# Attention output computed with channels on partitions and turned into a mirrored token order, and a Fourier mix that reads each frequency row twice

## The chip, the cores and the metric

The kernel runs on one core of a Trainium2 chip. The metric is device time in microseconds of one execution; below, a "profile" is one execution recorded by the hardware profiler, with the start, length and releaser of every instruction. The engines are TensorE (PE; its weight loads are recorded apart, as PEld), VectorE (DVE), ScalarE (ACT), GpSimd (POOL) and SyncE (SP), which here only issues transfers. Each engine executes its own list of instructions in the order in which it stands in the program.

## What is computed

A gated linear attention over 4 batches, 8 heads, 768 tokens and 48 channels a head, followed by one FNet block on the 4 x 768 x 384 result, all in float32:

```python
f = 1.0 / (1.0 + np.exp(-f_logit))
for t in range(S):
    state = f[:, :, t, :, None] * state + np.einsum('bhd,bhe->bhde', k[:, :, t], v[:, :, t])
    y[:, :, t] = np.einsum('bhd,bhde->bhe', q[:, :, t], state)
x = y.transpose(0, 2, 1, 3).reshape(B, S, H * D)
mixed = np.real(np.fft.fft(np.fft.fft(x, axis=1), axis=2))
u = x + mixed
un = (u - mean(u)) / np.sqrt(var(u) + 1e-06)          # over the last axis
out = u + np.maximum(un @ w_ch1, 0.0) @ w_ch2         # 384 -> 1536 -> 384
```

The weights arrive as float64 and are rounded to float32 on the chip.

## The kernel before

**Units.** `attention(u, x_all)` handles two heads of one batch; there are 16 units, four for each batch. Tokens lie along the row and channels on the partitions: head 0 on partitions 0 to 47, head 1 on 64 to 111, with zeros between (so 112 rows, `R`). A unit is a generator cut by `yield` into seven pieces: (0) the gates, a chain through DVE, ACT and POOL that ends in `wq`, `wk` and the scaled Q and K; (1) `sa`, (2) `sb`, (3) `sc`, (4) `sd`: score products of blocks of growing size on TensorE, with `double` on DVE in between, which folds the decay into Q and K; POOL and ACT copy the scores into `AT`; (5) `st` and `ds`: K's chunks are transposed (L262), copied to `kT` (L265, L266), multiplied with v (L269), and a chain of five DVE operations carries the state from chunk to chunk (L272, L274), on 96 columns of which each head uses its own 48; (6) `y`: for each of six chunks of 128 tokens, scores by v (L282) and Q by state (L286) give 128 tokens x 48 channels for each head; one ACT copy (L288) brings them to `x`, where tokens lie on partitions. After that the next transfer into this unit's `qkf` buffer is issued.

**FNet.** `fnet(b, x)` handles a batch in 18 pieces. Piece 1 forms `eo`, the sums (DVE, L300) and differences (POOL, L301) of tokens s and s + 384, and folds the channels around the middle into `xf` (L304 to L306). Pieces 2 to 4 compute `z`, channel terms by frequencies 0 to 384, in three groups of 128 rows (L321, L324); ACT copies each to `zz` (L326) and DVE makes `zr`, the same columns reversed and with a sign (L328), since frequency 768 - m is the mirror of m. Pieces 5 and 6 compute `mix`, six chunks of 128 tokens by 384 channels, from `zz` for the first three and from `zr` for the last three (L337); for each chunk DVE adds it to `x` and takes the statistics of the layer norm (L339 to L342), and after every three chunks ACT computes `rstd`. Then, in two halves of three chunks: `un` (DVE), its transposes `pt` (TensorE), the copy `unT` (ACT), twelve groups `up` with ReLU (L364, L367), three groups `po` (L375), the sum (L377), and a store on SP's queue (L378).

**Order.** The loop at the end runs in ticks. A unit starts every third tick and one piece of each running unit is written per tick; then two pieces of the work `behind`: first the 24 conversions of the weights, later `fnet` of a batch whose units are all done. The framework then orders each engine's instructions by its own estimate of when they can run, so that the list is near the written order, but not the same. Rotating buffers are the rest of the coupling: two PSUM tiles for the scores (`sc`), one for `y`, two for `fnet` (`f`), three `qkf` buffers.

## Time and profile before

| what | us |
|---|---|
| median of 3 runs | 943.72 |
| lowest, highest run | 943.67, 949.11 |
| span of the profiled execution, first to last instruction | 932.4 |
| TensorE busy, 9848 instructions | 741.6 (80%) |
| VectorE busy | 396.8 (43%) |
| GpSimd busy | 233.1 (25%) |
| ScalarE busy | 203.5 (22%) |

For the profiled execution only the span is given and no time of its own; the median is 11.3 us longer than it. "Busy" adds up the recorded lengths of an engine's instructions. In rows of groups, `out<-in` names the tiles, `128*64` for a matmul the rows and columns of the stationary operand, `128x193` the moving one, and `xN` how many instructions. What stands in brackets is how long the engine sat idle before, and who ended it. In a table by stage the first pair of numbers is the stretch, then its length, then the busy time (and number of instructions) of each engine; behind them stand the granted clock of TensorE, as a share of full speed, the transfers' share and GB/s.

### The profile page before, as it was taken

The numbers are of one execution on the slowest core, as the hardware profiler recorded it, in microseconds if no ns is written. First come the engines' busy times: TensorE is split into PE (matmuls) and PEld (weight loads), VectorE is DVE, ScalarE is ACT, GpSimd is POOL, SyncE is SP. The second block draws the span as 40 slices with busy tenths as digits, with TensorE's granted clock in tenths as the row PEclk, the third lists the DMA queues.
The fourth block names the chain that finished last, engine by engine and source line by source line (L and its number), as shares of the span: only waits on it lengthen the run. The fifth ranks groups of instructions, "written<-read, shape, count | busy, mean of one in ns | idle before, by whom it ended". The sixth has DMA issues, their size and how long they took to land.

```text
span 932.4 us, 21578 instructions
## 1 busy us (share of the span) xinstructions
PE 741.6 (80%) x9848; PEld 517.6 (56%) x9848; DVE 396.8 (43%) x739; ACT 203.5 (22%) x365; POOL 233.1 (25%) x246
## 2 busy tenths in 40 slices
PE   0352514447989989978999899869899999699998
PEld 0342403346765665666656656667656656555554
DVE  5977778676671131258721411465710211340000
ACT  2412121231242131213221311213320110112020
POOL 4556485554420020025210100144110000100000
PEclk9999999999979989968989889859899999799999
DMA  9224242402200200311201102022000000000000
GB/s 175 108 69 120 69 103 74 98 2 53 53 2 1 68 11 1 69 43 21 52 1 39 40 1 55 24 53 40 3 1 9 18 1 18 9 1 1 25 1 25
DMA packets 12075, 36.31 MB, mean 39 GB/s; under 512 B 1745, under 2 KB 5073, under 8 KB 10321
## 3 DMA queue, kind: packets, MB, share of 16 engines
q1 hardware_dynamic: 11984, 34.94, 15.5%
q8 instruction: 77, 1.26, 0.6%
q14 instruction: 14, 0.11, 0.0%
HBM read 30.22 MB, written 4.72 MB: 37 GB/s over the span
## 4 chain that ended last, share of the span: by engine, by line
PE 63%; DVE 5%; ACT 4%; POOL 4%; issue 3%; POOLq 0%
PE up L364 21%; PE po L375 17%; PE y L282 5%; PE mix L337 4%; PE z L321 4%; PE y L286 2%; PE sb L187 2%; PE ds L269 2%; DVE qkf L207 1%; POOL gk L170 1%; POOL wk L176 1%; PE sa L187 1%; PE z L324 1%; PE st L262 1%; POOL eo L301 1%
## 5 line engine op out<-in xcount | busy, mean ns | idle before, releaser
L364 PE MATMUL up<-unT,w 128*128 128x384 f32 x576 | 197.8, 503 | 1.3 <-ACT unT L358 1.1
L375 PE MATMUL po<-w,h 128*128 128x384 f32 x576 | 192.1, 494 | 0.0
L364 PEld LDWEIGHTS up<-unT,w 128*128 128x128 f32 x576 | 111.2, 196 | 77.1 <-issue 6.1
L375 PEld LDWEIGHTS po<-w,h 128*128 128x128 f32 x576 | 110.5, 193 | 76.8 <-issue 3.2
L377 DVE TENSOR_TENSOR x<-po,x 128x384 f32<-128x384 f32 x24 | 13.3, 556 | 224.8 <-PE po L375 224.8
L207 DVE TENSOR_TENSOR qkf<-qkf,tl 112x384 f32<-112x384 f32 x64 | 52.3, 817 | 121.6 <-PE sb L187 95.0
L230 POOL COPY at<-ad 32x384 f32<-32x384 f32 x64 | 56.5, 883 | 164.7 <-DVE ad L192 162.7
L367 ACT ACTIVATE h<-up 128x384 f32<-128x384 f32 x96 | 47.2, 492 | 166.8 <-PE up L364 166.8
L282 PE MATMUL y<-v,at 128*128 128x48 f32 x384 | 76.0, 338 | 3.4 <-issue 3.4
L170 POOL TENSOR_TENSOR gk<-qkf 112x768 f32<-112x768 f32 x16 | 29.5, 1846 | 194.4 <-DVE qkf L160 162.3
L282 PEld LDWEIGHTS y<-v,at 128*128 128x128 f32 x384 | 66.2, 248 | 8.4 <-issue 3.7
L187 PE MATMUL sb<-qkf 48*32 48x32 f32 x3072 | 37.7, 221 | 22.5 <-DVE qkf L208 21.1
L286 PE MATMUL y<-stt,qkf 48*128 48x48 f32 x320 | 41.2, 341 | 14.9 <-DVE stt L272 9.5
L252 PE MATMUL sd<-qkf 48*64 48x64 f32 x384 | 19.1, 262 | 42.7 <-DVE qkf L208 42.7
L187 PEld LDWEIGHTS sb<-qkf 48*32 48x32 f32 x3072 | 32.7, 122 | 34.0 <-DVE qkf L208 25.9
L208 DVE TENSOR_TENSOR qkf<-qkf,tl 112x384 f32<-112x384 f32 x64 | 46.3, 724 | 0.0
L120 POOL TENSOR_TENSOR tailf<-tailf,pow 128x384 f32<-128x384 f32 x24 | 35.5, 1481 | 42.3 <-DVE pow L118 34.8
L321 PE MATMUL z<-tab,xf 128*128 128x193 f32 (+1 forms) x192 | 37.9, 372 | 8.9 <-POOL xf L306 8.9
L252 PEld LDWEIGHTS sd<-qkf 48*64 48x64 f32 x384 | 16.7, 172 | 48.3 <-issue 48.3
L286 PEld LDWEIGHTS y<-stt,qkf 48*128 48x128 f32 x320 | 30.2, 231 | 23.7 <-DVE stt L272 10.0
L176 POOL TENSOR_TENSOR wk<-wk,qkf 112x768 f32<-112x768 f32 x16 | 30.4, 1900 | 36.8 <-ACT wk L172 36.7
L288 ACT COPY x<-y 128x576 f32<-128x576 f32 x16 | 10.2, 639 | 134.3 <-PE y L286 134.3
(76 smaller groups left out, 889.4 us busy)
## 6 DMA issues: line engine op xcount, KB each, us to landing
qkf<-in_qkf_dram SPq DMA_DIRECT2D x32, 432.0 KB, 6.7
raw<-in_w_ch_dram SPq DMA_DIRECT2D x24, 384.0 KB, 3.3
v<-in_v_dram SPq DMA_DIRECT2D x16, 288.0 KB, 3.2
out_dram<-x SPq DMA_DIRECT2D x24, 192.0 KB, 1.9
tab<-in_seq_tab_dram SPq DMA_DIRECT2D x1, 1158.0 KB, 15.6
cd<-in_dim_tab_dram SPq DMA_DIRECT2D x1, 576.0 KB, 15.7
masks<-in_sel_dram SPq DMA_DIRECT2D x1, 64.0 KB, 5.8
ident<-in_ident_dram SPq DMA_DIRECT2D x1, 64.0 KB, 5.8
```

The costliest lines, as they stand in the source:

```text
L170: nc.gpsimd.tensor_tensor(blocks(gk), blocks(g), at(g, LEAF - 1), ALU.subtract)
L176: nc.gpsimd.tensor_tensor(wk, wk, K, ALU.mult)
L187: nc.tensor.matmul(ps[32 * s:32 * s + 32, r, off + 32 * c:off + 32 * c + 32], lhsT=kk[ROWS[r], o:o + 32], rhs=qq[ROWS[r], o:o + 32], start ...
L207: nc.vector.tensor_tensor(qv[:, :, 1], qv[:, :, 1], wide(tv[:, :, 0:1]), ALU.mult)
L208: nc.vector.tensor_tensor(kv[:, :, 0], kv[:, :, 0], wide(tv[:, :, 1:2]), ALU.mult)
L230: nc.gpsimd.tensor_copy(AT[rows, :, :, 32 * s:32 * s + 32], AD[rows])
L282: nc.tensor.matmul(o, lhsT=AT[:, r, c], rhs=vt[:, c, r * D:(r + 1) * D], start=True, stop=(c == 0))
L286: nc.tensor.matmul(o, lhsT=Q[ROWS[r], c * C:(c + 1) * C], rhs=st[ROWS[r], c - 1, r * D:(r + 1) * D], start=False, stop=True)
L321: nc.tensor.matmul(o, lhsT=xf[:, i, j, ch], rhs=tab[:, j, cs, cols], start=(j == 0), stop=(j == 2))
L364: nc.tensor.matmul(pp[:, :3 * 128], lhsT=w1[:, kt, m * 128:(m + 1) * 128], rhs=unT[:, kt], start=(kt == 0), stop=(kt == 2))
L367: nc.scalar.activation(h, pp[:, :3 * 128], AF.Relu)
L375: nc.tensor.matmul(po[:, :DM], lhsT=h1[m][:, i * 128:(i + 1) * 128], rhs=w2[:, m], start=(m == 0), stop=(m == NF - 1))
```

## The change

1. *States.* `ds` and `st` hold only each head's own 48 columns: two matmuls of 64 and 48 weight columns for each chunk (`FILL`), and DVE operations of 48 columns for 96. The transposes are laid at steps of 128 columns, so that one ACT copy replaces two.
2. *Output.* `y` is computed with channels on the partitions and tokens along the row: v is now the stationary operand and `AT` the moving one (128 columns), then the state is stationary and Q moves. Head 0 goes to partitions 0 to 63, head 1 to 64 to 111. Two ACT copies bring it to `yT`, the second with the tokens 385 to 767 reversed. A new piece transposes six chunks (`yt`, in the score buffers) and ACT copies them to `x`. So in `x` chunk c + 3 holds, in row p, the mirror image of the token in chunk c; the slot that would be token 768 holds token 384. A unit has eight pieces.
3. *Fourier stages.* The folded channels are two tiles, `xc` (cosines) and `xs` (sines); even and odd frequencies stand side by side, so that a matmul streams 386 columns and not 193. POOL makes a copy of one chunk of sums, in which one element is the difference. `zr` and its DVE operations go. One frequency row in the middle is a group of its own (`mid`, one weight column). Each of three `mix` groups is used twice: as it is for chunk c, and with its columns read backwards (385 columns, column 0 again at the end) for chunk c + 3. The statistics of all chunks follow behind the three groups. `fnet` has 20 pieces.
4. *Store.* The chunks 0 to 2 are stored by SP as before; the mirrored chunks 3 to 5 by an indirect transfer of POOL with a table of row numbers, `place`, that two iotas write at the start.

```diff
-        for c in range(NCH - 1):
-            nc.tensor.matmul(ps[:R, 0, c * 2 * D:(c + 1) * 2 * D], lhsT=kT[:, c], rhs=vt[:, c],
-                             start=True, stop=True)
+            for r in range(2):
+                nc.tensor.matmul(ds[FILL[r], c], lhsT=kT[:, c, FILL[r]], rhs=vt[:, c, r * D:(r + 1) * D],
+                                 start=True, stop=True)
...
         for c in range(NCH):
             for r in range(2):
-                o = y[:, r, c * D:(c + 1) * D]
-                nc.tensor.matmul(o, lhsT=AT[:, r, c], rhs=vt[:, c, r * D:(r + 1) * D],
-                                 start=True, stop=(c == 0))
...
+                nc.tensor.matmul(y[FILL[r], c * C:(c + 1) * C],
+                                 lhsT=vt[:, c, r * D:r * D + (64 if r == 0 else D)], rhs=AT[:, r, c],
+                                 start=(c % 4 == 0), stop=(c == 0), skip_group_check=True)
+        for c in range(1, NCH):
+            for r in range(2):
+                nc.tensor.matmul(y[ROWS[r], c * C:(c + 1) * C], lhsT=st[ROWS[r], c - 1],
+                                 rhs=Q[ROWS[r], c * C:(c + 1) * C], start=False, stop=True,
+                                 skip_group_check=True)
+
+        yT = p2.tile([128, S], F32, tag="yT", name=f"yT{u}")[:R]
+        nc.scalar.copy(yT[:, :HS + 1], y[:R, :HS + 1])
+        nc.scalar.copy(yT[:, HS + 1:], y[:R, S - 1:HS:-1])
+        yield
+
+        ps = ps_a.tile([128, 2, 512], F32, tag="sc", name=f"yt{u}").rearrange("p a b -> p (a b)")
+        for c in range(NCH):
+            nc.tensor.transpose(ps[:, c * 128:c * 128 + R], yT[:, c * C:(c + 1) * C], ident[:R, :R])
+        nc.scalar.copy(
+            x_all[:, :, hp * 2 * D:(hp + 1) * 2 * D].rearrange("t c (r e) -> t c r e", r=2),
+            ps[:, :NCH * 128].rearrange("t (c r k) -> t c r k", r=2, k=64)[:, :, :, :D])
...
+    def store(b, c, rows):
+        if c < 3:
+            nc.sync.dma_start(out=out[b, c * C:(c + 1) * C], in_=rows)
+        else:
+            nc.gpsimd.indirect_dma_start(
+                out=out.rearrange("b s d -> (b s) d"),
+                out_offset=bass.IndirectOffsetOnAxis(ap=place[:, b, c - 3:c - 2], axis=0),
+                in_=rows, in_offset=None)
...
+        nc.gpsimd.tensor_tensor(o, x[:, 0:3], x[:, 3:6], ALU.subtract)
+        nc.gpsimd.tensor_copy(e[:, 3], e[:, 0])
+        nc.gpsimd.tensor_copy(e[0:1, 3], o[0:1, 0])
+        nc.vector.tensor_tensor(xs[:, :, 1:HD], o[:, :, 1:HD], o[:, :, DM - 1:HD:-1], ALU.subtract)
+        nc.vector.tensor_tensor(xc[:, :, 1:HD], e[:, :, 1:HD], e[:, :, DM - 1:HD:-1], ALU.add)
+        nc.gpsimd.tensor_copy(xc[:, :, 0:HD + 1:HD], e[:, :, 0:HD + 1:HD])
...
+            parts = []
+            if T < 2:
+                ch = slice(128 * T, 128 * T + 128)
+                parts += [(z[:, :2 * NQ], xc[:, j, ch], tab[:, j, 0]) for j in (1, 2)]
+                parts += [(z[:, EV], xc[:, 0, ch], tab[:, 0, 0, EV]), (z[:, OD], xc[:, 3, ch], tab[:, 0, 0, OD])]
+            if T == 1:
+                parts += [(z[64:128, :2 * NQ], xs[:, j, 0:64], tab[:, j, 1]) for j in range(3)]
+            if T == 2:
+                parts += [(z[:, :2 * NQ], xs[:, j, 64:192], tab[:, j, 1]) for j in range(3)]
...
-            nc.vector.tensor_scalar(zr[:, T], zz[:, T, S // 2:0:-1], sgn[:, T:T + 1], None, ALU.mult)
...
+        mid = mixed(f"mid{b}", slice(HS, HS + 1), DM)
+        row = p1.tile([128, DM], F32, tag="row", name=f"row{b}")
+        nc.vector.tensor_tensor(row[0:1], mid[0:1, :DM], x[0:1, 3], ALU.add)
+        for c in range(3):
+            mix = mixed(f"mix{b}_{c}", slice(c * 128, (c + 1) * 128), DM + 1)
+            nc.vector.tensor_tensor(x[:, c], mix[:, :DM], x[:, c], ALU.add)
+            nc.vector.tensor_tensor(x[:, c + 3], mix[:, DM:0:-1], x[:, c + 3], ALU.add)
+            if c == 0:
+                nc.vector.tensor_copy(x[0:1, 3], row[0:1])
+            yield
```

Where instructions stand changes in three places. In the names the number behind the letters is the unit (`sd11`) or the batch and group (`po1_5`, `z2_0`).

TensorE before, from the last `po` instruction of batch 1 to the first rows of the products that follow:

```order
L375 MATMUL po1_5_5099<-w2_89,h1_1_1_11_4990 128x384
L252 MATMUL sd11_5114<-qkf2_82 64x64 x12
L187 MATMUL sa12_5132<-wq12_5071,wk12_5072 32x32 x48
L187 MATMUL sa12_5132<-qkf0_80 32x32 x48
L262 MATMUL st11_5234<-ident_93,qkf2_82 128x112 x5
L282 MATMUL y11_5364<-v11_4079,at1_84 128x48 x4
L269 MATMUL ds11_5243<-v11_4079,kT11_5240 112x96 x5
L187 MATMUL sb12_5255<-qkf0_80 32x32 x48
L286 MATMUL y11_5364<-stt11_5249,qkf2_82 128x48 x2
```

Then follow the rest of y11 and sb12, sc12, sd12, sa13 and z2_0. TensorE after, from the last rows of y11, whose first rows now stand right behind the last `po1_5`:

```order
L300 MATMUL y11_5474<-qkf2_82,stt11_5329 48x128 x10
L245 MATMUL sc12_5500<-qkf0_80 32x32 x24
L311 MATMUL yt11_5548<-ident_94,yT11_5497 128x112 x6
L258 MATMUL sd12_5560<-qkf0_80 64x64 x12
L193 MATMUL sa13_5578<-wq13_5535,wk13_5536 32x32 x48
L193 MATMUL sa13_5578<-qkf1_81 32x32 x48
L275 MATMUL st12_5680<-ident_94,qkf0_80 128x112 x5
L361 MATMUL z2_0_5823<-tab_91,xc_87 128x386 x2
```

sd11, sa12, st11, ds11 and sb12 no longer stand between the batches, but between `up` and `po` of batch 1: st11 and ds11 behind po1_3.

POOL before, around the difference `eo` of batch 1:

```order
L211 TENSOR_TENSOR tl9_3770<-tl9_3770 112x6
L301 TENSOR_TENSOR eo1_3873<-x1_1663 128x1152
L230 COPY at0_83<-ad0_85 32x12x32 x4
L306 COPY xf_87<-eo1_3873 128x3x2 x2
L170 TENSOR_TENSOR gk10_4118<-qkf1_81 112x768
```

POOL after:

```order
L217 TENSOR_TENSOR tl9_3860<-tl9_3860 112x6
L236 COPY at0_83<-ad0_85 32x12x32 x4
L323 DMA out_0_dram<-x0_126,place_96 3072x384 x2
L337 TENSOR_TENSOR eo1_4097<-x1_1699 128x1152
L338 COPY eo1_4097<-eo1_4097 128x384
L339 COPY eo1_4097<-eo1_4097 1x384
L342 COPY xc_87<-eo1_4097 128x4x2
L176 TENSOR_TENSOR gk10_4175<-qkf1_81 112x768
```

The copies to `at0` moved ahead of the difference, two indirect stores stand between, and two copies follow it.

DVE before, in batch 3, from the third `mix` group on:

```order
L339 TENSOR_TENSOR x3_5007<-mix3_2_6904,x3_5007 128x384
L341 BN_STATS bs3_2_6909<-x3_5007 128x6
L342 BN_AGGR mv3_6886<-bs3_2_6909 128x2
L354 TENSOR_SCALAR un3_0_6941<-x3_5007,mv3_6886,rstd3_6887 128x384
L339 TENSOR_TENSOR x3_5007<-mix3_3_6914,x3_5007 128x384
L354 TENSOR_SCALAR un3_1_6948<-x3_5007,mv3_6886,rstd3_6887 128x384
```

DVE after, from the last `mix` group on:

```order
L384 TENSOR_TENSOR x3_4994<-mix3_2_7036,x3_4994 128x384
L390 BN_STATS bs3_2_7048<-x3_4994 128x6
L390 BN_STATS bs3_3_7053<-x3_4994 128x6
L391 BN_AGGR mv3_7015<-bs3_2_7048 128x2
L390 BN_STATS bs3_4_7056<-x3_4994 128x6
L391 BN_AGGR mv3_7015<-bs3_3_7053 128x2
L390 BN_STATS bs3_5_7059<-x3_4994 128x6
L391 BN_AGGR mv3_7015<-bs3_4_7056 128x2
L403 TENSOR_SCALAR un3_0_7065<-x3_4994,mv3_7015,rstd3_7016 128x384
```

Before, the first `un` stood ahead of the last three groups of `mix`; now it stands behind the last group and four statistics.

More of the change, by code (lines that the diff above doesn't have):

```diff
@@ L41 @@
     NQ = S // 4 + 1
+    HS = S // 2
     HD = DM // 2
@@ L276, in attention @@
         yield
[L278 removed]
+        y = ps_y.tile([128, 2, 512], F32, tag="y", name=f"y{u}").rearrange("p a b -> p (a b)")
         for c in range(NCH):
             for r in range(2):
[L281 to L287 removed]
@@ L332, in fnet, with mixed @@
         rstd = p2.tile([128, NCH], F32, tag="rstd", name=f"rstd{b}")
-        for c in range(NCH):
-            mix = ps_f.tile([128, 512], F32, tag="f", name=f"mix{b}_{c}")
-            src = zz if c < 3 else zr
-            for T in range(3):
-                nc.tensor.matmul(mix[:, :DM], lhsT=src[:, T, (c % 3) * 128:(c % 3 + 1) * 128], rhs=cd[:, T],
-                                 start=(T == 0), stop=(T == 2))
-            nc.vector.tensor_tensor(x[:, c], mix[:, :DM], x[:, c], ALU.add)
+        def mixed(name, rows, n):
+            mix = ps_f.tile([128, 512], F32, tag="f", name=name)
+            for T in range(3):
+                nc.tensor.matmul(mix[:rows.stop - rows.start, :n], lhsT=zz[:, T, rows], rhs=cd[:, T, :n],
+                                 start=(T == 0), stop=(T == 2))
+            return mix
+        mid = mixed(f"mid{b}", slice(HS, HS + 1), DM)
[8 more added lines that the diff above has]
+            yield
+        for c in range(NCH):
             bs = p3.tile([128, 6], F32, tag="bs", name=f"bs{b}_{c}")
@@ L377, in fnet @@
                 nc.vector.tensor_tensor(x[:, c], po[:, :DM], x[:, c], ALU.add)
-                nc.sync.dma_start(out=out[b, c * C:(c + 1) * C], in_=x[:, c])
+                store(b, c, x[:, c])
                 yield
-    left, xs, active, behind = [HP] * B, {}, [], [weights()]
+    left, xs_of, active, behind = [HP] * B, {}, [], [weights()]
     u = tick = 0
@@ L396 @@
                 if not left[b]:
-                    behind.append(fnet(b, xs.pop(b)))
+                    behind.append(fnet(b, xs_of.pop(b)))
         for _ in range(BESIDE):
```

80 lines of the change are left out of this document (33 added, 47 removed).

## The prediction

> **What bounds the kernel now.** I read the page's first line, then a table of busy time by stage. TensorE (PE, its weight loads PEld beside it) is the engine that carries the second half, so I cut the span where its work changes kind: up to the first Fourier matmul `z` of batch 0; then for each batch from `z` to the first `up`; from `up` to the last `po`; and the gap from there to the next batch's `z`.
>
> ```profile
> span 932.4 us, 21578 instructions
> core 0: us, PE busy (x) PEld busy (x) DVE busy (x) ACT busy (x) POOL busy (x), PEclk, DMA share, GB/s
> 0.00:227.20 227.20, 87.59 (x2709) 77.73 (x2709) 169.46 (x309) 55.22 (x88) 128.41 (x123) 1.00 0.36 89
> 227.20:273.98 46.78, 44.32 (x658) 34.38 (x658) 31.21 (x62) 16.70 (x30) 13.24 (x14) 0.87 0.13 27
> 273.98:395.90 121.92, 119.35 (x1075) 75.12 (x1075) 26.51 (x52) 25.29 (x46) 13.60 (x21) 0.95 0.12 29
> 395.90:427.18 31.28, 21.46 (x732) 19.67 (x731) 21.08 (x33) 5.57 (x10) 14.08 (x13) 0.62 0.21 47
> 427.18:470.86 43.68, 40.62 (x658) 30.54 (x658) 30.29 (x60) 16.65 (x30) 12.84 (x14) 0.91 0.14 29
> 470.86:593.80 122.94, 119.95 (x1076) 75.79 (x1076) 26.51 (x52) 25.32 (x46) 13.60 (x21) 0.95 0.12 28
> 593.80:625.88 32.08, 21.85 (x733) 19.88 (x732) 20.05 (x30) 5.55 (x10) 13.80 (x13) 0.59 0.20 45
> 625.88:671.79 45.91, 42.83 (x659) 32.56 (x658) 31.11 (x62) 16.59 (x30) 13.16 (x13) 0.87 0.12 22
> 671.79:791.65 119.86, 117.24 (x1076) 73.43 (x1078) 18.84 (x41) 17.54 (x36) 5.79 (x13) 0.97 0.03 9
> 791.65:808.45 16.80, 7.72 (x84) 6.77 (x83) 7.21 (x13) 2.12 (x4) 4.36 (x2) 0.78 0.04 13
> 808.45:833.23 24.78, 23.89 (x106) 16.15 (x106) 9.92 (x24) 3.42 (x9) 0.19 (x1) 0.94 0.00 1
> 833.23:932.40 99.17, 94.74 (x297) 55.56 (x297) 4.61 (x9) 13.56 (x29) 0.00 (x0) 1.00 0.03 12
> ```
>
> The first stage is VectorE's (169 of 227 us busy; TensorE 88). From there TensorE is busy 95 to 98% in every long stage, so an instruction taken off it there is time. The exceptions are the gaps of 31.28 and 32.08 us: TensorE is busy 21.5 us, and at a granted clock of 0.62 and 0.59. There only attention runs, and the next batch's `z` waits for it.
>
> The prices of TensorE work, from its own timeline (start, length, group; a group's length holds the drain of its last one, so I take starts where I can; a float32 matmul shows as two instructions, a transpose as one):
>
> ```profile
> 309.85 0.42 PE L286 MATMUL y<-stt,qkf 48*128 48x48 f32 x4
> 310.20 0.65 PE L282 MATMUL y<-v,at 128*128 128x48 f32 x4
> 310.78 0.42 PE L286 MATMUL y<-stt,qkf 48*128 48x48 f32 x4
> 332.61 0.87 PE L357 MATMUL pt<-ident,un 128*128 128x128 f32 x6
> 395.90 0.91 PE L252 MATMUL sd<-qkf 48*64 48x64 f32 x24
> 396.74 0.99 PE L187 MATMUL sa<-wq,wk 48*32 48x32 f32 x94
> 795.30 1.22 PE L269 MATMUL ds<-v,kT 128*112 128x96 f32 x10 [0.36 <-ACT kT L265]
> 808.45 5.14 PE L321 MATMUL z<-tab,xf 128*128 128x193 f32 x24 [7.43 <-POOL xf L306]
> 814.59 1.58 PE L321 MATMUL z<-tab,xf 128*64 128x193 f32 x12
> 819.23 5.97 PE L337 MATMUL mix<-cd,zz 128*128 128x384 f32 x18
> 825.04 5.97 PE L337 MATMUL mix<-cd,zr 128*128 128x384 f32 x18
> ```
>
> 18 `mix` instructions take 825.04 - 819.23 = 5.81 us, 0.323 each or 0.841 ns a column. Four L286 and four L282 take 0.93.
>
> **The change, part by part.** *Fourier stages.* `z` ran 10.8 us (808.45 to 819.23). Now it has 4, 7 and 3 matmuls which stream 1158, 2316 and 1158 columns; twice 4632 by 0.841 ns is 7.8: -3.0. `mix` had 36 instructions, 11.6 us; `mid` and three `mix` have 24, 7.75: -3.9. Batches 0 to 2 lie under a busy TensorE: 3 x -6.9 = **-20.7**.
>
> *Attention output.* Before, a unit's `y` is 20 L286 and 24 L282: 5 x 0.93 + 0.57 = 5.2 us (four more L282 from 310.20 to 310.78), and `ds` 1.2. Now 24 instructions load 64 or 48 columns, stream 128, and go by turns to the two column halves. Nearest row: `z` 128*64, 1.58 / 12 = 0.132 for 193 columns, under the 0.162 that 193 columns cost in one stream, so the halves overlap. Scaled to 128 columns: 0.087 x 24 = 2.1. The 20 state instructions use both diagonal quarters; `sd` (two row halves by turns, 64 columns) costs 0.91 / 24 = 0.038, doubled for 128 columns: 1.5. `ds` is 20 small ones at 0.038: 0.8. Six transposes by the `pt` row (0.145): 0.9. Sum 5.3 against 6.4, **-1.2** a unit, and 12 units lie in busy stages (the first four are under VectorE): **-14.4**. Bounds: 0.054 (128 columns, halves fully side by side) to 0.145 (the `pt` row) for each of the 44; that is -15 to +33 us on the total.
>
> *Order and gaps.* A unit now has one piece more, `fnet` two more, so a batch's pieces fill ten of its twelve ticks and not nine. TensorE's order shows it: sd11, sa12, st11, ds11 and sb12 stand ahead of po1_5 and no longer behind it. Work in the gap was sd 0.8, sa 1.9, st 0.7, ds 1.2, sb 1.9, y 5.2, sc 0.5, sd 0.8, sa 1.9 = 14.9 us (sa, sb and sc have 192, 192 and 48 instructions at the L187 row's 0.01; st's 0.67 is quoted further down), so 16.4 of 31.28 was waiting or a slow clock. Now: y 3.6, sc 0.5, yt 0.9, sd 0.8, sa 1.9, st 0.7 = 8.4. Its length is set by the chain to `z`:
>
> ```profile
> L326 ACT COPY zz<-z 128x386 f32<-128x386 f32 x12 | 5.8, 482 | 41.1 <-PE z L321 33.2 <-PE z L324 7.9
> L230 POOL COPY at<-ad 32x384 f32<-32x384 f32 x64 | 56.5, 883 | 164.7 <-DVE ad L192 162.7
> 416.96 3.78 POOL L301 TENSOR_TENSOR eo<-x 128x1152 f32<-128x1152 f32 x1 [6.34 <-ACT x L288]
> 801.07 0.64 ACT L288 COPY x<-y 128x576 f32<-128x576 f32 x1 [5.57 <-PE y L286]
> 801.85 3.71 POOL L301 TENSOR_TENSOR eo<-x 128x1152 f32<-128x1152 f32 x1 [40.89 <-ACT x L288]
> 805.60 1.42 DVE L304 TENSOR_TENSOR xf<-eo 128x573 f32<-128x573 f32 x2 [2.50 <-POOL eo L301]
> 807.75 0.93 POOL L306 COPY xf<-eo 128x6 f32<-128x6 f32 x2 [2.19 <-DVE xf L305]
> ```
>
> y 3.6; two turned copies on ScalarE by the 0.482 row, 1.1 with the hand-over; yt 0.9; copy to `x` 0.7; GpSimd's subtraction 3.8; its two new copies (row 0.883 for 384 elements) 1.8; `xc`, 764 elements at 1.42 / 1146, 1.0; the edge copy 0.4: 13.3. In the gaps of before the part from subtraction to `z` took 10.2 us (416.96 to 427.18) against 6.6 at the end (801.85 to 808.45), because copies of `at` and VectorE's doublings came between; the copies now stand ahead, so I add 2, not 3.6: 15.5. Waiting falls from 16.4 to 7.1, -9.3 in each of two gaps: **-18.6**. The third gap had 7.9 us of work in 16.80; now 4.5 in 13.3: 0. Queued behind the new wait of yt for ScalarE are sd, sa, st, which `z` doesn't need.
>
> *Junction before the second half's `up`.* It held this:
>
> ```profile
> 336.05 0.67 PE L262 MATMUL st<-ident,qkf 112*128 112x112 f32 x5 [2.57 <-DVE qkf L208]
> 336.56 1.50 PE L282 MATMUL y<-v,at 128*128 128x48 f32 x8
> 337.86 2.15 PE L269 MATMUL ds<-v,kT 128*112 128x96 f32 x10
> ```
>
> 2.57 idle, then a slow clock: y 1.50 for 1.15, ds 2.15 for 1.22. That is 3.9 a batch. st and ds now stand between `po` groups; in their place yt and three `pt` wait for ScalarE's copies, which I put at 1.0. **-8.7** in three batches; bounds 0 gained (and the wait in all 12 units: +21) to -12.
>
> *First stage.* fnet 0 starts a tick later, but `z` keeps its place behind sa5. Added: turned copies 1.0, yt about 1.2 by the slow `st`-like pace; x's subtraction now behind `at` copies, 0.9: **+3**. Bounds -3 (y itself is shorter) to +10 (a whole tick, a third of 31.28). The iotas, memsets and the copy to `cd` on GpSimd lie ahead of or behind gk0 in idle time; 0.
>
> *End.* Batch 3 is alone, so all counts: `z` -3.0, `mix` -3.9. Against it the statistics:
>
> ```profile
> 831.04 0.56 DVE L339 TENSOR_TENSOR x<-mix,x 128x384 f32<-128x384 f32 x1 [0.56 <-PE mix L337]
> 831.52 0.47 DVE L354 TENSOR_SCALAR un<-x,mv,rstd 128x384 f32<-128x384 f32 x1
> 831.91 0.55 DVE L341 BATCH_NORM_STATS2 bs<-x 128x6 f32<-128x384 f32 x1
> 832.49 0.18 DVE L342 BATCH_NORM_AGGREGATE mv<-bs 128x2 f32<-128x6 f32 x1
> out_dram<-x SPq DMA_DIRECT2D x24, 192.0 KB, 1.9
> ```
>
> Before, `up` began 2.2 us after the last `mix` (831.04 to 833.23), three chunks' statistics done long ahead. Now VectorE does two additions (1.1), four statistics (2.2), four short aggregates (0.7), three `un` (1.4) behind it, then a transpose and a copy (0.9): 6.1 with overlaps, +3.9. The last store is a scatter from GpSimd where SP's landed in 1.9; the trace has no scatter, bounds 0 to 3.8 (the longest GpSimd row), I take the middle, +2. Sum **-1**. [...] The other eleven scatters have idle GpSimd time around them (0.0 to 14.1 us busy a stage) and stand ahead of work that waits for `x` anyway.
>
> Sum: -20.7 - 14.4 - 18.6 - 8.7 + 3 - 1 = -60.4. Against the profiled span: 932.4 - 60.4 = 872.0. The median of 943.72 lies 11.3 above that span; I add the same: **883 us**.
>
> **Rivals.** A, *halves don't overlap*: each of the 44 output instructions costs the `pt` row's 0.145. 12 x (24 x 0.058 + 20 x 0.069) = +33: 916. [...] The 0.132 for 193 columns speaks against it; that row has runs of six in one half, so it doesn't exclude it. B, *yt stalls TensorE*: no gain at the junctions, and every unit shows 1.06 us of ScalarE copies: 8.7 + 12.7 = +21, 904. For it: yt stands one 0.6 us group behind `y`; against: `pt` lies between in half the places. C, *scatter holds GpSimd*, the slower one: in each of three gaps the subtraction stands behind two scatters in GpSimd's queue and is ready 6.4 us in. With T us each from 0.6 us on, it loses 2T - 5.8 in each and T - 2 at the end; 7T = 80 decides, T = 11.4. At 13 us: 955. The longest GpSimd row, 3.78 us for 1152 elements a partition, speaks against. D, *gaps stay*: VectorE's gate chain, not the missing cover, sets them: +19, 902.
>
> **How the numbers follow.** Forecast 0.57; A 0.13; B 0.12; D 0.10; C 0.04; two of A, B, D at once (937 or so) 0.04. The range goes from 862 (the low bounds of y and of the first stage, -21) to 916 (A), leaving out C, the pairs and the worse half of A, 0.15. About 1% is what a measurement of this kernel tells from none: faster 0.92, same 0.04, slower 0.04.
>
> **What would show it.** The same table after: gaps 1 and 2 near 15 us at a higher clock; `up` to `po` near 114; `z` 7.8 and `mid` with `mix` 7.75 in the last batch; last `mix` to `up` near 6. Wrong if y's 24 instructions take over 3 us, if a scatter shows more than 3 us on GpSimd ahead of `eo`, or if the first stage passes 232.

## The result, and the profile after

The changed kernel takes 884.9 us, the median of 4 runs (882.84 to 885.2); before it was 943.69 over 4 runs (938.39 to 949.11). The ratio is 0.9416, with a 95% interval of 0.9359 to 0.9473 (the two medians alone give 0.938). The forecast was 883 us, faster. The total holds; most of the sum under it does not, as the experiments show. Every table and row below comes of one profiled execution of each kernel. For the kernel before that was a quick one: its span is 932.4 us, and the four timed executions above have spans of about 936 to 947.

The first lines of the page of the changed kernel:

```profile
span 880.8 us, 21805 instructions
PE 675.0 (77%) x9928; PEld 435.8 (49%) x9928; DVE 381.1 (43%) x727; ACT 213.1 (24%) x381; POOL 251.4 (29%) x266
```

The table of busy time by stage, cut at the same events and with the same columns as the one of before (first `z`, first `up`, end of the last `po`):

```profile
0.00:232.23 232.23, 77.33 (x2778) 62.80 (x2778) 163.62 (x308) 58.21 (x92) 131.96 (x128) 0.86 0.36 87
232.23:283.23 51.00, 44.58 (x1003) 29.37 (x1001) 37.67 (x77) 20.41 (x36) 17.74 (x22) 0.83 0.24 49
283.23:396.14 112.91, 111.54 (x1165) 68.50 (x1164) 28.90 (x54) 25.82 (x47) 18.18 (x24) 0.99 0.08 21
396.14:409.90 13.76, 8.13 (x321) 7.15 (x320) 9.10 (x10) 3.12 (x6) 7.88 (x5) 0.80 0.45 102
409.90:454.18 44.28, 39.27 (x1002) 26.85 (x1001) 37.14 (x77) 20.29 (x36) 17.73 (x22) 0.96 0.27 56
454.18:570.93 116.75, 113.10 (x1166) 69.30 (x1164) 28.86 (x54) 25.87 (x47) 18.08 (x24) 0.98 0.08 20
570.93:583.34 12.41, 8.60 (x321) 7.08 (x320) 8.39 (x9) 3.60 (x7) 7.91 (x5) 0.81 0.52 114
583.34:632.92 49.58, 42.73 (x1001) 28.39 (x1001) 37.77 (x77) 19.96 (x36) 17.73 (x22) 0.88 0.10 21
632.92:741.66 108.74, 108.16 (x782) 65.62 (x780) 12.63 (x30) 17.19 (x35) 4.17 (x6) 0.98 0.03 10
741.66:752.96 11.30, 3.64 (x52) 2.95 (x51) 3.89 (x4) 1.50 (x3) 7.07 (x5) 0.83 0.05 17
752.96:777.52 24.56, 20.34 (x61) 10.79 (x62) 9.38 (x25) 3.89 (x10) 0.00 (x0) 0.85 0.00 0
777.52:880.80 103.28, 97.61 (x297) 56.95 (x297) 3.74 (x7) 13.20 (x27) 2.95 (x3) 0.96 0.03 12
```

The three gaps lost 17.5, 19.7 and 5.5 us, the long stretches from `up` to `po` 9.0, 6.2 and 11.1. But the stretches from `z` to `up`, from which the prediction took 6.9 us of TensorE's work, did not become shorter: 51.00, 44.28 and 49.58 after 46.78, 43.68 and 45.91. The last stage grew by 4.1, the first by 5.0. Together -51.6.

What the last batch does alone, from TensorE's timeline (start, length, group, idle time ahead and what ended it):

```profile
741.66 1.52 PE L295 MATMUL y<-at,v 128*64 128x128 f32 x24
743.11 1.29 PE L300 MATMUL y<-qkf,stt 48*48 48x128 f32 x20
744.99 0.89 PE L311 MATMUL yt<-ident,yT 112*128 112x112 f32 x6 [0.58 <-ACT yT L305]
752.96 5.66 PE L361 MATMUL z<-tab,xc 128*128 128x386 f32 x16 [7.08 <-POOL xc L342]
758.55 4.30 PE L361 MATMUL z<-tab,xs 128*64 128x386 f32 x12
762.78 2.10 PE L374 MATMUL mid<-cd,zz 128*1 128x384 f32 x6
764.81 6.10 PE L374 MATMUL mix<-cd,zz 128*128 128x385 f32 x18
774.54 2.41 PE L406 MATMUL pt<-ident,un 128*128 128x128 f32 x9 [3.63 <-DVE mv L391]
...
777.52 26.35 PE L413 MATMUL up<-unT,w 128*128 128x384 f32 x72 [0.57 <-ACT unT L407]
```

Two long waits stand here, 7.08 us for `xc` and 3.63 for the statistics. What follows each is slow: `z` takes 9.82 us (752.96 to 762.78) for a forecast 7.8, and 72 `up` take 26.35, where the second half's 72 take 23.49. In quarters of a microsecond the granted clock reads 0.50 from 749.25 to 756.0 and from 773.25 to 783.25.

### The profile page after: what moved, and what is told of

The parts are those of the page before. It is cut to its first block, busy times and chain, and to the rows that moved or that the text cites. A ratio compares the mean times of both kernels' runs of the same rounds, so it can differ in the third digit from the quotient of the medians.

```text
span 880.8 us, 21805 instructions
## 1 busy us (share of the span) xinstructions
PE 675.0 (77%) x9928; PEld 435.8 (49%) x9928; DVE 381.1 (43%) x727; ACT 213.1 (24%) x381; POOL 251.4 (29%) x266
## 3 DMA queue, kind: packets, MB, share of 16 engines
q1 hardware_dynamic: 10368, 32.58, 15.8%
q8 instruction: 78, 1.28, 0.6%
## 4 chain that ended last, share of the span: by engine, by line
PE 58%; DVE 8%; ACT 4%; issue 3%; POOL 3%; DMA 0%; POOLq 0%
PE up L413 21%; PE po L424 20%; PE z L361 4%; PE sa L193 2%; POOL gk L176 1%; PE sb L193 1%; PE y L300 1%; PE ds L282 1%; PE mid L374 1%; PE y L295 1%; DVE qkf L214 1%; DVE qkf L213 1%; PE pt L406 1%; DVE qkf L183 1%; PE sd L258 1%
## 5 line engine op out<-in xcount | busy, mean ns | idle before, releaser
L424 PEld LDWEIGHTS po<-w,h 128*128 128x128 f32 x576 | 108.1, 190 | 72.3
L323 POOL DMA_INDIRECT out_dram<-x,place x12 | 12.1, 1010 | 241.9 <-DVE x L426 241.9
L176 POOL TENSOR_TENSOR gk<-qkf 112x768 f32<-112x768 f32 x16 | 39.8, 2490 | 144.5 <-DVE qkf L166 90.1
L236 POOL COPY at<-ad 32x384 f32<-32x384 f32 x64 | 46.7, 729 | 68.7 <-DVE ad L198 66.7
L213 DVE TENSOR_TENSOR qkf<-qkf,tl 112x384 f32<-112x384 f32 x64 | 47.4, 741 | 32.8 <-issue 17.8
L300 PE MATMUL y<-qkf,stt 48*48 48x128 f32 x320 | 27.7, 312 | 27.1 <-DVE stt L287 17.6
L305 ACT COPY yT<-y 112x385 f32<-112x385 f32 x16 | 7.7, 478 | 166.8 <-PE y L300 166.8
L193 PE MATMUL sa<-wq,wk 48*32 48x32 f32 x1536 | 19.8, 223 | 34.6 <-POOL wk L182 29.9
L214 DVE TENSOR_TENSOR qkf<-qkf,tl 112x384 f32<-112x384 f32 x64 | 43.6, 682 | 0.0
L198 DVE COPY_PREDICATED ad<-masks,sa 128x384 f32<-128x384 uint32 x32 | 18.6, 583 | 41.1 <-PE sa L193 41.1
L193 PEld LDWEIGHTS sa<-wq,wk 48*32 48x32 f32 x1536 | 16.8, 123 | 39.4 <-POOL wk L182 30.4
## 6 DMA issues: line engine op xcount, KB each, us to landing
cd<-in_dim_tab_dram SPq DMA_DIRECT2D x1, 576.0 KB, 18.6
```

The source lines that it names most:

```text
L176: nc.gpsimd.tensor_tensor(blocks(gk), blocks(g), at(g, LEAF - 1), ALU.subtract)
L193: nc.tensor.matmul(ps[32 * s:32 * s + 32, r, off + 32 * c:off + 32 * c + 32], lhsT=kk[ROWS[r], o:o + 32], rhs=qq[ROWS[r], o:o + 32], start ...
L213: nc.vector.tensor_tensor(qv[:, :, 1], qv[:, :, 1], wide(tv[:, :, 0:1]), ALU.mult)
L214: nc.vector.tensor_tensor(kv[:, :, 0], kv[:, :, 0], wide(tv[:, :, 1:2]), ALU.mult)
L236: nc.gpsimd.tensor_copy(AT[rows, :, :, 32 * s:32 * s + 32], AD[rows])
L300: nc.tensor.matmul(y[ROWS[r], c * C:(c + 1) * C], lhsT=st[ROWS[r], c - 1], rhs=Q[ROWS[r], c * C:(c + 1) * C], start=False, stop=True, skip ...
```

## The account by work, clock and waiting

In half microseconds the granted clock reads 1.00 or 0.50, with little between: 1605 and 233 of 1864 before, 1480 and 258 of 1761 after. So I cut each span from 225 us on, up to the last whole half microsecond, into half microseconds and counted three things: TensorE's idle time; its busy time times one minus the granted clock (what the half clock cost, taking all work to run in proportion); and the rest, its work at full clock.

| kernel | work at full clock | lost to half clock | idle | sum, us |
|---|---|---|---|---|
| before | 605.7 | 49.7 | 51.6 | 707.0 |
| e1: before, new pieces | 607.9 | 53.5 | 43.1 | 704.5 |
| e2: e1 with the new Fourier stages | 588.8 | 57.9 | 40.3 | 687.0 |
| e3: e1 with the new output | 589.7 | 15.8 | 45.5 | 651.0 |
| after (both) | 570.7 | 29.8 | 55.0 | 655.5 |
| e9: before, y streams twice the columns | 612.1 | 30.3 | 52.6 | 695.0 |

From before to after the sum falls by 51.5: 35.0 of it is work and 19.9 half clock, and waiting went up by 3.4. The parts differ far more than that, as the rows of e1 to e3 show.

The account has two limits. In the changed kernel the column reads 1.00 up to its first change at 165.5 us, whatever the pace: 24 `sd` take 1.55 us at 95.48, where it reads 1.00, and 1.54 at 190.40, where it reads 0.50, while they take 0.92 at 400.71, where it reads 1.00 again. So I leave the first stage out. In the kernel before the first change comes at 248 us, and its first `z` is slow (12 instructions in 3.95 us, 227.20 to 231.15); by the same estimate up to 3 us of its work there are half clock. And the small matmuls slow down less than in proportion: in the changed kernel 96 `sb` take 1.22 us at 169.82, where the column reads 0.50, and 1.02 at 238.96, where it reads 1.00. The split between the first two columns is therefore rough by some us; the sum is not.

## Experiments

Each run was timed beside the kernel before on its own chip, and the medians differ: the kernel before took 940.02 us beside e1 to e4, 937.55 beside e5, e7, e8 and e9, and 938.84 beside e6, e11 and e13. So across chips the ratios compare, and the times only roughly.

**The change in its parts.** e1 cuts the kernel before into as many pieces as the changed one; e2 and e3 add one half of the change to e1.

```diff
 # e1, on before
+        yield                      # between y's matmuls and the copy to x
         nc.scalar.copy(x_all[...], y[...])
...
-                yield
+            if c % 3:
+                yield              # behind mix 1, 2, 4 and 5
```

> The kernel before, its arithmetic unchanged, cut into pieces as the changed one is: a unit of attention in 8 pieces (the copy of y to x is a piece of its own), fnet in 20 (a piece ends after mix 1, 2, 4 and 5). Theory of the prediction (the order gives the gaps and the junctions): gaps 1 and 2 lose 9 us each or more, the junction ahead of the second up 2.9 in three batches, 943.7 - 27 = 916. Rival (the gaps shrank because there was less work in them): gaps within 3 us of 31 and 32, total 938 to 944.

> The changed kernel with the attention output, the states and kT of the kernel before (tokens on partitions), in the same 8 and 20 pieces. Its x is not mirrored, so chunks 3 to 5 of the output hold other sums; the amount of work is that of the folded Fourier stages. Theory of the prediction: order -27, Fourier -20.7, end -1: 895. If the new output is worth what the rows of the changed kernel show (4.1 us of TensorE a unit for 6.4, 12 units, -28) this run lacks that: 885 + 28 = 913. Rival (the output is a loss or worth nothing): 885 or less.

> The kernel before with the new states, output, turned copies and yt transposes, in 8 and 20 pieces; kT and yT have one buffer and not two, for lack of room. Its x is mirrored and its Fourier stages don't know it, so all the output holds other sums; plain stores. Theory of the prediction: order -27, output -14.4, first stage +3: 905. By the rows of the changed kernel (-28 for the output): 891 to 894. Rival (the gain is in the Fourier stages): 930 or more.

Measured: before 940.02 on that chip; e1 931.82 (ratio 0.9931, 0.9897 to 0.9966), e2 915.4 (0.9777, 0.9709 to 0.9845), e3 878.15 (0.9378, 0.9312 to 0.9445). All three sums that follow the prediction missed (916, 895 and 905); for e2 the second one, 913, which takes the output's worth from the changed kernel's rows, came near. The order is worth 2.5 us of span (932.4 to 929.9), or 8.2 by the medians of 13 and 10 executions (interval 3 to 10); not 27, and not the 0 to 6 of the rival either. The output, on top of it, is worth 53.7 (to 876.2). The Fourier stages are worth 17.8 with the old output (912.1) and nothing with the new one: e3 without them has a shorter span than the changed kernel, 876.2 for 880.8, and the intervals of the two ratios overlap. Taken in the other order, the output is worth 31.3 behind the Fourier stages (912.1 to 880.8). So the two halves don't add up: each takes part of the other's gain.

The stage table of e1 shows where the order's 27 us went; first cycle, from `z` over `up` to the next `z`:

```profile
228.59:285.35 56.76, 52.97 (x934) 40.03 (x933) 37.10 (x75) 18.31 (x33) 16.41 (x22) 0.85 0.18 39
285.35:408.96 123.61, 120.19 (x1217) 75.63 (x1218) 30.42 (x56) 26.09 (x48) 15.92 (x22) 0.94 0.09 21
408.96:424.23 15.27, 10.30 (x315) 9.47 (x313) 9.75 (x12) 2.33 (x4) 4.56 (x3) 0.68 0.41 92
```

The gap fell to 15.27, to a few tenths what the prediction said. But the stretch from `z` to `up` went from 46.78 to 56.76 (and the next one, behind the gap, from 43.68 to 53.39). The order moved the gap's work across its borders, where it took as long. Against the profiled execution of before only 8.5 us of idle time went, and 2.2 of work with 3.8 of half clock came.

e3's gain has another make-up: 18.2 us less work (the prediction's 14.4) and 37.7 less lost to half clock.

**Why the old output lowers the clock.** In the kernel before, the clock falls to 0.50 behind a unit's `y` although TensorE has no idle time there. Rows of 2 us, TensorE's busy time first, the clock third from the right:

```profile
308.00:310.00 2.00, 2.00 (x20) 1.78 (x20) 0.56 (x1) 0.00 (x0) 0.00 (x0) 1.00 0.21 77
310.00:312.00 2.00, 2.00 (x20) 1.78 (x20) 0.00 (x0) 0.00 (x0) 0.00 (x0) 1.00 0.09 29
312.00:314.00 2.00, 2.00 (x55) 1.42 (x54) 1.03 (x2) 1.47 (x3) 0.00 (x0) 0.75 0.57 174
314.00:316.00 2.00, 2.00 (x4) 1.06 (x4) 0.00 (x0) 0.00 (x0) 0.00 (x0) 0.50 1.09 245
316.00:318.00 2.00, 2.00 (x7) 1.04 (x6) 0.00 (x0) 0.00 (x0) 0.00 (x0) 0.90 0.88 171
```

From 308 to 312 stands `y`: 128 weight columns loaded for 48 columns streamed. Then 48 `po` take 17.44 us, and the clock reads 0.50 from 313.0 to 316.25. The first stage has the same in the lengths, where the column reads 1.00. From 205.02 to 217.3 TensorE has no idle time, and its last `y` groups there still take the lengths that such groups have where the column reads 0.50 (1.09 and 0.67 from 408.33 on; 0.65 and 0.42 at 1.00, from 308.92 on):

```profile
214.87 1.09 PE L282 MATMUL y<-v,at 128*128 128x48 f32 x4
215.88 0.67 PE L286 MATMUL y<-stt,qkf 48*128 48x48 f32 x4
```

e9 makes `y` stream more for the same loads:

```diff
-                o = y[:, r, c * D:(c + 1) * D]
+                n = D if r and c == NCH - 1 else 2 * D
+                o = y[:, r, c * D:c * D + n]
-                nc.tensor.matmul(o, lhsT=AT[:, r, c], rhs=vt[:, c, r * D:(r + 1) * D], ...)
+                nc.tensor.matmul(o, lhsT=AT[:, r, c], rhs=vf[:, (2 * c + r) * D:(2 * c + r) * D + n], ...)
...                                      # the same for Q by state
```

> The kernel before; each matmul of y streams 96 columns in place of 48, the second 48 give sums that the next chunk's matmuls overwrite. More work, no other change. Theory (the granted clock falls where TensorE streams few columns for each weight load, even while it is busy, and that is what the old output cost): TensorE time at half clock falls, the loss to it from 50 to 20 to 35 us, and the kernel is faster, 915 to 935. Rival (only idle time lowers the clock): 44 instructions a unit up to 0.04 us longer, 12 units: 943 to 965.

Measured: 922.75 for 937.55, ratio 0.9855 (0.9802 to 0.9909). With twice the columns in `y` the kernel is 1.5% faster, and the interval leaves out 1. The same place in e9:

```profile
303.27 0.47 PE L290 MATMUL y<-stt,qkf 48*128 48x96 f32 x4
303.67 0.69 PE L284 MATMUL y<-v,at 128*128 128x96 f32 x4
...
308.21 15.75 PE L379 MATMUL po<-w,h 128*128 128x384 f32 x48
```

```profile
303.00:305.00 2.00, 2.00 (x17) 1.45 (x15) 0.56 (x1) 0.00 (x0) 0.00 (x0) 1.00 0.09 27
...
309.00:311.00 2.00, 2.00 (x8) 1.21 (x7) 0.35 (x1) 0.29 (x1) 0.00 (x0) 1.00 1.28 324
```

`y` itself is longer (1.01 us for eight, 0.93 before), the clock stays at 1.00, and 48 `po` take 15.75. Nor is it the transfers: they are as heavy in e9 at full clock (1.28 of the DMA column) as in before at half clock (1.09). The whole kernel does 6.4 us more work and loses 19.4 less to half clock. So in these two kernels TensorE's clock answers to how much it streams (0.50 behind a `y` of 48 columns, 1.00 behind one of 96), and not only to how busy the profile calls it. Whether it counts columns for each load or columns in a time, no run here tells apart. e9 takes away 19.4 us of the 37.7 by which e3 loses less than e1; what in the new output takes away the rest (its `ds`, its longer streams, its shorter units) is not shown. By the account, half clock cost 49.7 of the 932.4 us of the kernel before, 5.3%.

**The halves of the array by turns.** e4 swaps the two loops of `y` (all of head 0, then all of head 1).

```diff
-        for c in range(NCH):
-            for r in range(2):
+        for r in range(2):
+            for c in range(NCH):
                 nc.tensor.matmul(y[FILL[r], ...], ...)
```

> The changed kernel with the 24 value and the 20 state matmuls of an output unit in another order: first all of head 0, then all of head 1, not by turns. Theory (the halves of the array overlap only where neighbours use different ones): 24 instructions from 0.060 to 0.108 us each (128 columns at 0.841 ns), 20 from 0.061 to 0.108: +2.1 us a unit, 12 units under a busy TensorE, 885 + 25 = 910, and more in the gaps. Rival (a matmul of 64 weight columns is that fast in any order): 885 within 3.

Measured: 886.0, ratio 0.946 (0.9388 to 0.9532); no difference that the intervals can tell, so the time went with the rival. The instructions did get slower, nearly as expected; from e4's timeline, beside the 1.52 and 1.29 of the changed kernel:

```profile
744.62 2.44 PE L295 MATMUL y<-at,v 128*64 128x128 f32 x24
746.99 1.99 PE L300 MATMUL y<-qkf,stt 48*48 48x128 f32 x20
```

From start to start, 24 instructions take 2.37 us for 1.45, 0.099 each for 0.060, both at a clock of 1.00. One stream of 128 columns costs 0.108 by the 0.841 ns a column: so by turns the halves overlap, and without turns hardly. The slower instructions add 20.3 us of work from 225 us on (591.0 for 570.7). But 8.8 less were lost to half clock and 6.5 less were idle, most of this in the first stage, which was 4.7 shorter; the span is only 4.9 longer (885.7). Why the first stage was shorter is open.

**These two waits cost more than their length.** e6 fills the last batch's two waits with matmuls that nobody reads.

```diff
+            for i in range(9):     # behind yt, last unit
+                nc.tensor.matmul(warm[:, :384], lhsT=yT[:, 0:128], rhs=yT[:, 384:768], start=True, stop=True)
...
+                for i in range(4): # behind mix 2, last batch
+                    nc.tensor.matmul(warm[:, :384], lhsT=x[:, 2, 0:128], rhs=x[:, 2], start=True, stop=True)
```

> The changed kernel with matmuls that nobody reads in two waits of the last batch: nine of 384 columns behind yt, where TensorE waits 7.1 us for xc, and four behind the last addition of mix 2, where it waits 3.6 us for the statistics. Theory (such a wait costs more than its length, because TensorE comes out of it at half the granted clock): z 9.8 -> 7.9 us, the first half's 72 up 26.2 -> 23.4, last gap as long as it was; from the last gap to the end 139.1 -> 134.5, the kernel 4 us shorter, 881. Rival (the slow rows come of something else in those stretches): z and up as before, or longer, 885 to 887.

Measured: 878.12, ratio 0.9331 (0.9284 to 0.9378). TensorE in e6:

```profile
749.43 5.98 PE L318 MATMUL warm<-yT 112*128 112x384 f32 x18
756.68 4.14 PE L365 MATMUL z<-tab,xc 128*128 128x386 f32 x16 [1.27 <-POOL xc L346]
760.75 4.30 PE L365 MATMUL z<-tab,xs 128*64 128x386 f32 x12
764.99 2.10 PE L378 MATMUL mid<-cd,zz 128*1 128x384 f32 x6
```

`z` takes 8.31 us for 9.82 (the clock from `z` to `up` is 1.00 for 0.85), and the stretch from the last gap to the end 134.0 for 139.1 (745.38 to 879.40; 741.66 to 880.80), as the theory said. By the account that stretch lost 5.6 us to half clock in the changed kernel and nothing in e6. So the half clock behind the two waits cost 5 us in this batch, and it is a cost of the waits. The span as a whole is only 1.4 us shorter (879.4 for 880.8), since everything ahead of the last batch, which the edit leaves as it was, took 3.7 longer in this execution.

**Where the Fourier stages' saving goes.** TensorE's longest waits in the changed kernel that name the statistics (line, what ended them, us in total, times, longest):

```profile
PE sd L258 <- ACT rstd L395: 4.5, 3, 1.5
PE pt L406 <- DVE mv L391: 3.6, 1, 3.6
...
PE sc L245 <- DVE mv L391: 2.0, 3, 0.7
```

Together 10.1 us; e3 has none of them. A larger wait names nothing: from 227 us on, TensorE stands 17.7 us in seven places within `sa` (e3 14.6 in six, before 8.4 in four). Its cause is open, and it is part of the changed kernel's 55.0 us of idle time. e5 sets the statistics between the additions and the second half's behind the first feed-forward; e13 takes them out, from the changed kernel and from e8 (the new output with the old Fourier stages, x in token order).

```diff
 # e5
             nc.vector.tensor_tensor(x[:, c], mix[:, :DM], x[:, c], ALU.add)
+            stats(c)
             nc.vector.tensor_tensor(x[:, c + 3], mix[:, DM:0:-1], x[:, c + 3], ALU.add)
...
 # e8
-        nc.scalar.copy(yT[:, HS + 1:], y[:R, S - 1:HS:-1])
+        nc.scalar.copy(yT[:, HS + 1:], y[:R, HS + 1:S])
 # e13, both
-            nc.vector.bn_stats(bs, x[:, c])
-            nc.vector.bn_aggr(mv[:, c], bs)
...                                      # and both operations of rstd
```

> The changed kernel; the statistics of chunk c stand directly behind its addition, rstd of the first half behind chunk 2, the statistics of chunks 3 to 5 behind the first half's feed-forward. Theory (the Fourier stages lose their saving because TensorE waits for six chunks of statistics at once and then starts up at half the granted clock): last mix to up in the last batch 6.65 -> 4, in the others the waits for rstd and mv (7 us over three batches) go, and up's first 48 instructions run 15.8 for 16.8 to 18.2; 885 - 10 to - 15 = 870 to 875. Rival (VectorE's load in that stage decides, whatever the order): 882 to 886.

> The kernel before with the new states, output and yt transposes in 8 and 20 pieces, but with yT not turned, so that x is in token order and the old Fourier stages fit: the whole computation. Theory (the new output carries the gain, by TensorE's clock): as e3, 876 to 880. Rival (e3's time came of its wrong x): no difference expected from data, any time above 885 would say so.

> The changed kernel without the statistics: mean and reciprocal deviation are constants, so all the output is scaled otherwise; the rest as it was. Theory (the new Fourier stages save TensorE 7 us a batch, and the statistics, which now come all at once behind them, take it back): the stretch from z to up falls by 5 or more in each batch, total 860 to 866. Rival (the saving is lost elsewhere): 875 to 881, as much as the same edit brings to e8.

> The kernel e8 (new output, old Fourier stages) without the statistics, in the same way. Theory: there most of them ran beside the next mix, so little falls: 870 to 875, and the changed kernel without statistics is now the faster of the two by 8 or more, where with them it was 6 slower. Rival: the distance between the two stays as it was.

Measured: e5 888.37 (0.948, 0.943 to 0.953), a miss. The stretches from `z` to `up` fell by 7.8 in three batches, but those from `up` to `po` grew by 12.6, with 24 `up` at 10.81 us behind a wait where 8.01 is usual; in the last batch VectorE's list still had four statistics ahead of the first `un`, so the edit did not do there what it was for. e8 gave 879.28 (0.9406, 0.9346 to 0.9466), as expected and as e3: the old Fourier stages with the new output are as fast as the changed kernel, and compute the whole. Without statistics the changed kernel takes 874.98 (0.9311, 0.9267 to 0.9355) and e8 879.99 (0.9352, 0.93 to 0.9403). Both missed their totals: 860 to 866 was expected of the changed kernel without statistics, whose rival began at 875, and 870 to 875 of e8 without them. In the profiled executions e8 gains 0.4 us of span by the edit (877.4 to 877.0) and the changed kernel 11.2 (880.8 to 869.6); but 869.6 is the quickest of its four, the others have 871.7 to 874.6, so some 10 us is the fairer figure. The intervals of the changed kernel with and without statistics don't overlap, those of e8 do. The stretches from `z` to `up` of the changed kernel fell by 6.1, 2.7, 3.3 and 2.6 us, 5 or more only in the first batch; e8's grew by 2.3 in all. First and last stretch from `z` to `up` of the changed kernel without statistics:

```profile
232.27:277.20 44.93, 38.78 (x909) 25.35 (x907) 33.49 (x62) 18.47 (x31) 17.94 (x21) 0.94 0.24 50
...
747.16:769.15 21.99, 20.80 (x61) 11.05 (x61) 6.00 (x13) 2.88 (x6) 0.00 (x0) 0.86 0.00 0
```

So the saving is real, 19.0 us of work (589.7 for e3, 570.7 after), and the statistics that now come all at once take back about half of it. That the changed kernel would be the faster one without them was expected by 8 us or more; it is 5 in the medians of one chip, whose intervals overlap, so this flip is likely and not shown. Without statistics the account still has 21.0 us at half clock and 52.0 idle, for 15.8 and 45.5 in e3. What takes that rest, some 12 us, stays open.

**The chain to z.** e7 takes GpSimd's subtraction out of what the first `z` waits for.

```diff
+        nc.scalar.copy(e[:, 3], e[:, 0])
+        nc.vector.tensor_tensor(e[0:1, 3], x[0:1, 0], x[0:1, 3], ALU.subtract)
         nc.vector.tensor_tensor(xc[:, :, 1:HD], ..., ALU.add)
+        nc.gpsimd.tensor_tensor(xs[:, :, 1:HD], ..., ALU.subtract)
```

> The changed kernel; between x and the first z the copies go to ScalarE, the one turned element is a subtraction of one row on VectorE, and xs follows on GpSimd, so that z waits for the sum, a copy, a row and xc, no longer for GpSimd's 3.8 us subtraction. Theory: x to z 7.0 -> 4.5 in the last gap, as much in the others, three gaps, and a shorter time at half clock: 885 - 8 = 877. Rival (z then waits for something else, st or sa in TensorE's own queue): gaps 1 and 2 unchanged, 883.

Measured: 886.84 (0.9464, 0.9417 to 0.9511); the last gap 11.38 for 11.30, the others 14.86 for 13.76 and 12.73 for 12.41. A miss, and for the last gap its timeline says why:

```profile
750.22 3.77 POOL L337 TENSOR_TENSOR eo<-x 128x1152 f32<-128x1152 f32 x1 [3.07 <-ACT x L312]
752.10 2.30 DVE L339 TENSOR_TENSOR eo<-x 1x384 f32<-1x384 f32 x1 [0.58 <-ACT eo L338]
754.07 1.59 POOL L342 TENSOR_TENSOR xs<-eo 128x573 f32<-128x573 f32 x1
754.44 2.04 DVE L340 TENSOR_TENSOR xc<-eo 128x764 f32<-128x764 f32 x1
```

VectorE's subtraction of a single row runs beside GpSimd's and ends 0.41 us behind it, 2.30 us for 0.54 in the first gap, and `xc` takes 2.04 beside the next GpSimd operation, 0.95 in the first gap. The chain is free of GpSimd in the code, not on the chip. In the first gap the rival holds: `sa` and `st` stand ahead of `z` in TensorE's list, and `sa` waits 6.35 us there, up to 410.25, when `xc` was done at 409.76. The changed kernel has the same wait (5.25 us, up to 408.11), and `z` starts at 409.90, 1.45 us after `xc` is done.

**What e6 and e7 taught, put into e8.** e11 is e8 with VectorE and ScalarE alone in the last batch's chain, and seven filling matmuls behind the last `yt`.

```diff
-        nc.gpsimd.tensor_tensor(eo[:, 1], x[:, 0:3], x[:, 3:6], ALU.subtract)
+        (nc.vector if last else nc.gpsimd).tensor_tensor(eo[:, 1], x[:, 0:3], x[:, 3:6], ALU.subtract)
...
-            nc.gpsimd.tensor_copy(xf[:, i, :, 0:DM + 1:DM], eo[:, i, :, 0:HD + 1:HD])
+            (nc.scalar.copy if last else nc.gpsimd.tensor_copy)(xf[:, i, :, 0:DM + 1:DM], eo[:, i, :, 0:HD + 1:HD])
```

> The kernel e8 (new output in token order, old Fourier stages, the whole computation) with two edits in the last batch: the subtraction ahead of xf on VectorE and the edge copies on ScalarE, none on GpSimd, and seven matmuls that nobody reads behind the last yt. Theory: last gap 11.7 -> 10.2, z to up 26.0 -> 24.4: 876. Rival (GpSimd's subtraction ran beside other work, the clock doesn't matter): 879 to 880.

Measured: 877.35, ratio 0.9327 (0.9284 to 0.9369); the last gap 9.23 for e8's 11.70, the stretch from `z` to `up` 23.68 for 26.01.

```profile
753.03 4.03 PE L346 MATMUL z<-tab,xf 128*128 128x193 f32 x24 [0.43 <-ACT xf L331]
762.71 5.97 PE L362 MATMUL mix<-cd,zz 128*128 128x384 f32 x18
```

By the medians it is 7.5 us under the changed kernel, and e6 6.8, but the kernel before, too, took 4.9 less beside them (938.84 for 943.69). The intervals of both overlap the changed kernel's, and e11's overlaps e8's, so only the two shorter stretches are shown, and a shorter time is likely.

## Why the prediction held, and where it did not

The forecast is right as a sum of errors that cancel.

| step | predicted | in the spans |
|---|---|---|
| order: gaps -18.6, junctions -8.7 | -27.3 | -2.5 (e1) |
| output -14.4, first stage +3 | -11.4 | -53.7 (e3 after e1) |
| Fourier stages -20.7, end -1 | -21.7 | +4.6 (after, from e3) |
| span | -60.4 | -51.6 |
| from span to time | +11.3 | +4.1 |

The right column takes the three parts in one order and from one execution each, of two chips. By medians the order shows -8.2 (940.02 to 931.82) and the whole -58.8 (943.69 to 884.9). With the Fourier stages ahead of the output, the spans show -17.8 and -31.3 for the two.

- *Order.* The gaps themselves came out about as said (13.76, 12.41 and 11.30 for 15.5, 15.5 and 13.3, at a clock of 0.80 to 0.83), and ahead of the second half's `up` the 2.57 us wait shrank to 0.27. The step that failed is "Waiting falls from 16.4 to 7.1": it took all that was not work in a gap as waiting that cover would remove. Only 9.8 of it was idle time (31.28 less 21.46), 5.0 in e1 (15.27 less 10.30), and the rest a slow clock (0.62 there, 0.68 in e1), which went along with the work into the next stage. There is a slip in the sum besides: 13.3 and 2 are 15.3, not 15.5, which makes 0.4 us in two gaps.
- *Output.* The work was mis-sized a little: 24 value instructions 1.45 us (said 2.1), 20 state ones 1.22 (1.5), `yt` 0.7 (0.9), `ds` 0.7 (0.8); -18.2 in all for -14.4. The failure is the price of the old `y`: "5 x 0.93 + 0.57" is from a place at full clock, and neither the places at half clock nor what `y` did to the clock of the work behind it stood in the sum: -37.7 by the account, about half of it by e9 a matter of the streamed columns. The bound of -15 was exceeded by far.
- *Fourier stages.* 19.0 us of work went where -6.9 in each of four batches, 27.6, was said. The mis-sized term is `z`, "10.8" to 7.8: the 10.8 stand behind a wait of 7.43 us and hold half clock (0.50 up to 811.25). Behind a filled wait, at 1.00, the same old `z` takes 9.68 us (e11, 753.03 to 762.71) and the new one 8.31 (e6), so the work saved is 1.4 and not 3.0. "Batches 0 to 2 lie under a busy TensorE" is the step that failed: that stretch waits for the statistics too, for which only the last batch had a term.
- *End.* Last `mix` to `up` took 6.65 us for a forecast 6.1. Not foreseen were the slow rows behind the two waits, some 5 us by e6. A scatter holds GpSimd 1.0 us and lands 2.6 after its issue (medians of twelve); from the last `po` to the end it is 4.8 us for 3.5 before (876.01 to 880.80; 928.86 to 932.40), +1.3 for +2.
- *First stage.* +5.0 for +3, within its bounds; at 232.23 us it just passes the 232 that the prediction named as a sign of being wrong. Ahead of the first `z`, TensorE waits 2.81 and 2.46 us in `sa` for something that the profile doesn't name, but that is not the difference: e3 waits 2.61 and 1.92 us at the same place and reaches `z` at 227.13. With the new Fourier stages the first `z` stands at 234.08 in e2, and yet at 227.56 in e4, whose edit is in `y` alone. So what makes the extra time is open.
- *From span to time.* The 11.3 were no overhead. Each run's time is about 2 us over its own span (882.84 and 880.8). So the profiled execution of before took about 934.4 us, less than any of its four timed ones (938.39 to 949.11). Adding the difference of 11.3 added 9 us of chance, which happened to cover the 8.8 by which the span was missed. That the total came out at 884.9 for 883 is luck.
- *Rivals.* A is out: 0.060 us by turns and 0.099 without, both under its 0.145, and the pair of the changed kernel and e4 shows the two column halves to overlap by turns. B is out: `yt` waits 0.6 us once. C is out with a scatter of 1.0 us. D was wrong for the gaps, which closed; that closing them is worth little (e1) is what its number said, for another reason than its own.

## What to carry to other kernels

Before pricing TensorE's work by rows, look at the granted clock in small windows behind it: behind the `y` of the kernel before, which loads 128 weight columns for 48 streamed ones, it read 0.50 for some 3.3 us (313.0 to 316.25), so what such a group costs stands in other lines than its own. A gap that closes is not a gain until the stretch next to it is added; sum whole cycles. And where work is taken from one engine, check that what is queued behind it in that stretch (here six chunks of statistics) does not end last anyway. When a forecast adds a run's overhead to a profile's span, take both from the same execution.

## What the chip showed unexpectedly

- More multiplication made the kernel faster (e9: `y` streams 96 columns for 48; ratio 0.9855), and matmuls that nobody reads took 5 us off the last batch (e6, 134.0 for 139.1).
- A product of VectorE's slowed down beside GpSimd's subtraction, while the sum that starts 0.06 us ahead of the subtraction took 1.36 us all four times. From the timeline of the changed kernel: the same product of 112x384 takes 0.56 us alone, and 2.97 next to the subtraction, where it ends 0.4 us behind it:

```profile
399.49 0.56 DVE L213 TENSOR_TENSOR qkf<-qkf,tl 112x384 f32<-112x384 f32 x1 [2.68 <-PE sc L245]
401.41 3.78 POOL L337 TENSOR_TENSOR eo<-x 128x1152 f32<-128x1152 f32 x1 [3.35 <-ACT x L312]
402.63 2.97 DVE L213 TENSOR_TENSOR qkf<-qkf,tl 112x384 f32<-112x384 f32 x1
```
